# Chunk-selecting attention and a spatial gating unit on one core: dummy matmuls one by one, and a new table of order and engines

## The chip, the cores and the metric

The kernel runs on one core of a Trainium2 chip. The metric is the device time of one execution in microseconds. Engines are named as the profile names them: PE (TensorE's matmuls), PEld (its weight loads), DVE (VectorE), ACT (ScalarE), POOL (GpSimd), SP (SyncE, which here only issues DMAs).

## The reference

Attention in which each query looks at six chunks of 32 keys, picked by an upper bound of the score, followed by a gated MLP with a matrix over the sequence. Four batches, 8 heads, 768 positions, head width 64; MLP widths 512 and 1024.

```python
k_min = np.min(k_chunks, axis=3)
k_max = np.max(k_chunks, axis=3)
ub = np.sum(np.maximum(q * k_min, q * k_max), axis=-1)      # per query and chunk
ub = np.where(causal, ub, -1000000000.0)
top_chunks = np.argsort(ub, axis=-1)[..., -top_k:]
...
scores = np.where(sel & causal_positions, scale * q @ k.T, -1000000000.0)
attn = softmax(scores);  x = attn @ v                        # (4, 768, 512)
...
h = np.maximum(x @ w_in, 0.0)
u, v = h[..., :512], h[..., 512:]
v_n = (v - mean(v)) / np.sqrt(var(v) + 1e-06)
v_s = np.einsum('ts,bsd->btd', w_spatial, v_n) + b_spatial[None, :, None]
out = (u * v_s) @ w_out
```

Inputs and output are float32; the kernel computes in float16 with float32 sums.

## The kernel before

The work falls into 16 pairs of heads, numbered 0 to 15, four to a batch, and an MLP for each batch, numbered 0 to 3. Pairs 0 to 3 are cut into two halves of the sequence, `a` (rows 0 to 383) and `b` (384 to 767), so that work can start on the first half. Every step is an operation with a name: kind, pair (and half), and a number where there are several. Those that the text speaks of are:

- `ld_k4`, `ld_q0a`, `ld_wv2`: a load from HBM into a staging tile (`early` for the halves, `st` for the rest), issued by SP. `w_v` and `w_u` are the two halves of `w_in`, in four pieces each; `ws` is the matrix over the sequence.
- `c_k4`, `c_wv2`, `c_v6`: the cast of what was loaded to float16 (line 315, in a helper). `c_s10` copies a query once more, for pairs 10 to 15.
- `t_k4`, `e_k4`: six (for a half, three) transposes by PE (L562), and the copy of their result from PSUM into the tile `kqT` (L313 on ACT, L315 on DVE).
- `kmm0_4`, `kmm1_4`: greatest and least key of each chunk (L594, DVE); `km0_4`, `km1_4`: a copy of these for each of the two heads; `rq1_4`: the query's negative part (L612).
- `ub4`: the bounds, by PE (L629, L634); `max4`, `sel4`, `grd4`: the sixth greatest bound, the choice and a guard column; `tsel4`, `es4`: transpose and copy of the choice.
- `sc4_0` to `sc4_2`: scores with the mask added by PE (L746, L759, L767; L781 for pairs 10 to 15); `exp4_00` and so on: their exponentials (L795, ACT), two to a group; `tri4_00`: the causal edge (L806, POOL); `av4_0`, `av4_1`: attention times values (L829); `rec4_0`, `nrm4_0`: division by the sum.
- `tx0a`, `ex0a` or `xx5`: the attention's output transposed into `xT`, by PE or by a DMA. `x_kq10`, `xs10`, `xg0_1` are such transposing DMAs for other tiles.
- `v0_0`, `u0_0` (L878): the two projections of a tile of 128 rows; `rv`, `ru` (L885 on ACT, L887 on DVE) their relu; `bn`, `ag`, `ln`, `rs`, `vn` the normalisation; `s0_0` (L928) the product over the sequence; `g0_0` (L932, DVE) the gate; `o0_0` (L964) the output projection, `eo0_0` its copy from PSUM and `so0_0` its store. For the last tile of batch 3 the output is made in two pieces of 256 columns, `o3_5` and `o3_6`.
- `preset_...`: memsets of tiles that are filled once.
- `w0` to `w3`: dummy matmuls of 512 columns, whose result nobody reads (L454). The tile that they read is set to zero by `zero` (L409, DVE), and they write to the same two PSUM tiles `sc` as the scores.

Nothing is decided while the kernel is built: a table written out by hand, `ORDER`, names every operation in turn. The letter ahead of the colon is its engine (P for PE, D for DVE, A for ACT, G for POOL, S for SP), the digits behind it the buffers that it takes. `replay` walks through the table, and each engine's queue gets its operations in that order and runs them strictly one after the other; between engines only the data and the buffers make an operation wait. The list of engines that an operation may run on stands in its definition (`cast`, `evac`, `turned`).

`WARM` gives the dummies by operation: nine in `w0`, three in `w1`, five in `w2`, two in `w3`. In the table `w3` and `w2` stand first, `w1` behind the first two groups of transposes, and `w0` behind `t_k1b`, ahead of `tsel1a`.

Of the kernel before, what the change touches and what calls it, by code (L numbers as in the profile page):

```python
# [14 lines left out]
P = 128  # L15
# [15 lines left out]
def t_act(n):  # L31
    return n / 1.2 + 55.0


def t_pool(n):
    return n * 0.92 + 100.0
# [108 lines left out]
WARM = (9, 3, 5, 2)  # L145
# [25 lines left out]
max2aD:0 sc1a_0P:10 e_k0bA: e_q0bD: kmm0_0bD:2 sel2aD:0 preset_vt0D: km1_1bG: km0_1bA: km1_3aA: c_q2bA:3 grd2aA:
ub3aP:2 t_k2bP:0 tsel2aP:1 max3aD:1 ld_v2aS:7 ld_k4S:0 c_k4G:0 ld_k8S:1 ld_k3bS:8 ld_v1aS:2 es2aD:2 sel3aD:0 av0aP:3
e_k2bD: rec0aD:0 kmm1_0bD: t_q2bP:1 t_q1bP:2 kmm0_2bD:0 nrm0aD:0 kmm1_2bD: preset_sna1G: km1_0bG: grd3aG: km0_0bG:
c_k3bG:2 c_v1aG:2 ld_v3aS:0 c_v3aG:0 km0_2bG: exp1a_01A:1 exp1a_00A: rq1_0bA:0 c_q3bA:3 e_q2bA: e_q1bA: sc2a_0P:01
tsel3aP:0 t_q3bP:1 ub0bP:2 t_k4P:3 es3aD:3 e_q3bD: exp2a_01A:2 exp2a_00A: av1aP:0 max0bD:0 rec1aD:1 preset_vt1D:
c_v2aG:1 t_k3bP:1 e_k4A:4 grd0bA:1 km1_2bA: e_k3bA: sel0bD: nrm1aD:1 rq1_1bD:1 sc3a_0P:10 exp3a_01A:3 exp3a_00A:
tsel0bP:3 es0bD:4 kmm0_3bD:1 kmm1_3bD: tx0aP:2 tx1aP:0 ub1bP:1 av2aP:3 ex0aA:0 rq1_2bA:0 km0_3bG: rq1_3bD:1 rec2aD:2
max1bD:1 nrm2aD:0 sel1bD:1 ld_k5S:2 ld_v1bS:1 ld_wv0S:3 c_k5G:1 ld_wv3S:4 ld_k6S:5 c_wv0G:0 c_k6G:3 km1_3bG: ld_q4S:6
sc0b_0P:01 ex1aD: grd1bA: ub2bP:2 exp0b_01A:4 exp0b_00A: av3aP:3 t_k5P:1 tsel1bP:0 max2bD:0 kmm1_4D:2 rec3aD:0
sel2bD:1 nrm3aD:1 e_k5A:5 es1bD:0 c_q4G:0 c_k8G:2 ld_wv1S:7 c_wv1G: ld_wv2S:0 c_wv2G: c_wv3G: ld_wu2S:2 c_wu2G:0  # L180
ld_q6S:3 ld_q5S:5 ld_wu1S:6 ld_wu0S:1 ld_q8S:7 ld_wu3S:0 sc0b_1P:10 ub3bP:2 tx3aP:1 tx2aP:3 t_q4P:0 ex3aD: kmm0_4D:
t_k8P:1 exp0b_10A:5 exp0b_11A: grd2bA: e_k8A:0 e_q4D: preset_snb0G: ex2aD: max3bD:1 kmm1_5D:0 sel3bD:0 sc1b_0P:10
tsel2bP:0 v0_2P:1 v0_0P:3 exp1b_00A:6 exp1b_01A: km1_4A:1 grd3bG: km0_4G: rv0_0A:0 c_v1bG: tsel3bP:2 preset_sn0G:
c_q5G:1 tri1b_00G: rq1_4D:0 rv0_2A:1 es2bD:1 c_wu0G: es3bD:2 bn0_2D:0 sc1b_1P:10 ub4P:0 max4D:0 grd4G:2 c_wu3G:
c_q6G:0 c_wu1D: exp1b_10A:0 exp1b_11A: tri1b_10G: v0_1P:3 t_q5P:2 t_k6P:1 rv0_1A:2 e_k6A:1 preset_vt5D: sel4D: e_q5D:
bn0_0D:1 ld_k9S:4 c_k9D:2 ag0_2D:0 kmm0_5D: rq1_5D:1 sc2b_0P:10 u0_0P:3 u0_1P:0 t_q6P:1 exp2b_00A:1 exp2b_01A:
sc2b_1P:10 e_q6A: u0_2P:2 tsel4P:1 preset_vt4G: ru0_0D:0 es4D:3 exp2b_10A:2 exp2b_11A: ru0_1A:1 ld_ws4S:2 ld_v0bS:5
ld_ws0S:5 ld_k7S:1 av1bP:3 ld_v2bS:4 ld_ws1S:6 c_ws4A:1 km0_5G:2 tri2b_00G: c_k7G:3 km1_5G: tri0b_10G: tri2b_10G:
c_v2bG: tri0b_00G: epsG:0 sc3b_0P:10 exp3b_01A:3 exp3b_00A: t_k9P:1 c_v0bG: c_q8G:0 ld_q7S:0 c_q7G:2 ld_v3bS:6
ru0_2D:2 rec1bD:1 nrm1bD:1 kmm0_6D:1 bn0_1D:2 tx1bP:2 ub5P:0 max5D:1 av2bP:3 rec2bD:2 nrm2bD:0 ag0_1D: sel5D:0 e_k9A:2  # L190
ex1bA: sc3b_1P:01 exp3b_11A:0 exp3b_10A: t_k7P:1 t_q7P:3 t_q8P:2 av0bP:0 e_q8A: e_k7A:3 kmm1_6D: e_q7D: rec0bD:0
nrm0bD:1 kmm0_8D:2 rq1_6D:0 sc4_0P:10 tx2bP:3 ex2bD: ag0_0D: exp4_00A:6 exp4_01A: ld_ws2S:3 ld_wo0S:4 c_v3bG: c_ws1G:3
km0_6G:4 tri3b_00G: tri3b_10G: av3bP:2 tws4P:0 rec3bD:1 ld_ws3S:1 c_wo0G: km1_6G: grd5A: ld_v4S:2 c_v4G:5 tws1P:1
tx0bP:3 sc4_1P:10 ews4D:0 ex0bD: nrm3bD:0 c_ws0A:2 ln0_0A:0 ews1D: ld_ws5S:7 ld_q9S:0 ld_q11S:6 tri4_00G: c_ws5G:0
# [24 lines left out]
tri9_20G: sc10_0P:10 exp10_00A:6 v1_1P:1 av9_1P:3 av9_0P:2 rs1_1A: exp10_01A: ru1_3A:7 rv1_1A:3 sc10_1P:10 exp10_11A:0
# [55 lines left out]
def kernel(  # L275
# [760 lines left out]
```

## Time and profile before

| | us |
|---|---|
| median of three runs | 196.98 |
| lowest, highest | 196.94, 198.55 |
| the profiled execution, device time | 197.43 |
| its span, first to last instruction | 195.6 |
| PE busy in the span | 186.6 |
| DVE busy | 157.4 |
| ACT busy | 146.6 |
| POOL busy | 94.2 |

An engine's busy time counts its instructions on the engine; waiting, branching and issuing of DMAs is left out. Matmuls overlap one another, and the record of each holds its way through the array, so PE counts as busy while it is not at its full rate. A line such as L315 is that of a helper that many operations share.

### The profile page before, as it was taken

How to read it: one execution, taken by the hardware profiler on the slowest of the kernel's cores; microseconds unless marked ns; L12 is line 12 of the kernel's file. 1: busy time of each engine (PE TensorE's matmuls, PEld its weight loads, DVE VectorE, ACT ScalarE, POOL GpSimd, SP SyncE). 2: the span in 40 equal slices, each digit the busy share in tenths (PEclk: the TensorE clock that was granted, in tenths of full speed). 3: DMA queues.
4: the chain of work that ended last, by engine and by line, in shares of the span. 5: the costliest groups of instructions: out<-in, count | busy, mean ns of one | idle time of the engine just before them, and what ended most of it. 6: DMA issues, size and time to landing. Idle time of an engine off the chain costs nothing.

```text
span 195.6 us, 5812 instructions
## 1 busy us (share of the span) xinstructions
PE 186.6 (95%) x2201; PEld 107.9 (55%) x2201; DVE 157.4 (80%) x490; ACT 146.6 (75%) x231; POOL 94.2 (48%) x192
## 2 busy tenths in 40 slices
PE   7899979999999999999999999999999999999992
PEld 3457644576745646554357667566556654444441
DVE  5899988988998997995898997679947467895350
ACT  2699989999989997897999997788899330453142
POOL 4479469769688299932862674233615210000000
PEclk9999999999999999999999999999999999999999
DMA  5999899999999859999999989999171363812555
GB/s 145 326 336 285 282 302 278 323 350 352 275 227 220 137 135 245 190 244 179 257 212 225 264 161 159 272 261 218 57 167 57 80 138 107 229 41 111 165 180 192
DMA packets 98139, 41.01 MB, mean 210 GB/s; under 512 B 85440, under 2 KB 92864, under 8 KB 98112
## 3 DMA queue, kind: packets, MB, share of 16 engines
q1 hardware_dynamic: 97968, 40.52, 83.9%
q8 instruction: 17, 0.28, 0.6%
q10 hardware_dynamic: 144, 0.13, 0.2%
q14 instruction: 10, 0.08, 0.2%
HBM read 24.38 MB, written 6.29 MB: 157 GB/s over the span
## 4 chain that ended last, share of the span: by engine, by line
PE 69%; DMA 11%; POOL 8%; DVE 4%; issue 3%; SPq 2%; ACT 1%; POOLq 0%; ACTq 0%; DVEq 0%
PE gen L878 17%; PE gen L928 16%; PE gen L964 10%; PE gen L829 9%; PE sc L781 7%; DMA st<-in_moe_w_spatial_dram 5%; PE sc L746 4%; POOL n L315 3%; PE sc L759 3%; DMA early<-in_q_dram 2%; DMA early<-in_v_dram 2%; PE gen L629 2%; DMA st<-in_q_dram 1%; POOL vt L315 1%; SPq L515 1%
## 5 line engine op out<-in xcount | busy, mean ns | idle before, releaser
L795 ACT ACTIVATE e<-sc 128x768 f16<-128x768 f32 (+1 forms) x96 | 83.2, 916 | 12.6 <-PE sc L781 6.7
L806 POOL TENSOR_SCALAR_AFFINE_SELECT e<-e 128x512 f16<-128x512 f16 (+1 forms) x44 | 27.3, 630 | 23.2 <-ACT e L795 18.5
L928 PE MATMUL gen<-vn,wsT 128*128 128x512 f16 x144 | 34.2, 379 | 0.1
L594 DVE TENSOR_REDUCE kmm<-kqT 128x24 f16<-128x768 f16 (+1 forms) x40 | 30.3, 778 | 1.1 <-ACT kqT L313 1.1
L829 PEld LDWEIGHTS <-e 128*128 128x128 f16 x672 | 23.1, 97 | 4.3 <-issue 1.4
L932 DVE SCALAR_TENSOR_TENSOR late<-gen,bcol,u 128x512 f16<-128x512 f32 x24 | 17.7, 747 | 9.7 <-PE gen L928 9.7
L829 PE MATMUL gen<-vt,e 128*128 128x65 f16 x672 | 24.7, 193 | 0.6 <-DVE wsT L315 0.3
L964 PE MATMUL gen<-w_out,late 128*128 128x512 f16 (+1 forms) x100 | 23.8, 371 | 0.0
L928 PEld LDWEIGHTS <-wsT 128*128 128x128 f16 x144 | 13.3, 97 | 14.7 <-issue 0.6
L746 PE MATMUL sc<-kqT 64*128 64x128 f16 (+2 forms) x212 | 17.3, 271 | 0.6 <-ACT e L795 0.6
L896 DVE BATCH_NORM_STATS2 stats<-vraw 128x6 f32<-128x512 f32 x24 | 16.1, 684 | 1.8 <-ACT vraw L885 1.7
L313 ACT ACTIVATE late<-gen 128x512 f32<-128x512 f32 (+2 forms) x17 | 9.9, 587 | 9.6 <-PE gen L964 8.4
L781 PE MATMUL sc<-kqT,early 128*128 128x256 f16 (+2 forms) x132 | 16.7, 268 | 0.0
L885 ACT ACTIVATE vraw<-gen 128x512 f32<-128x512 f32 x14 | 8.2, 607 | 11.4 <-PE gen L878 11.3
L313 ACT ACTIVATE kqT<-gen 128x384 f16<-128x384 f16 (+1 forms) x21 | 12.6, 632 | 4.6 <-PE gen L562 4.4
L878 PEld LDWEIGHTS <-early 128*128 128x128 f16 x96 | 9.0, 98 | 10.8 <-issue 0.8
L656 DVE MAX8 max<-gen 128x8 f32<-128x20 f32 (+4 forms) x160 | 14.8, 166 | 0.0
L964 PEld LDWEIGHTS <-late 128*128 128x128 f16 x100 | 9.3, 97 | 9.6 <-issue 0.5
L878 PEld LDWEIGHTS <-xT 128*128 128x128 f16 x96 | 8.7, 97 | 9.2 <-issue 1.1
L315 POOL CAST n<-st 128x768 f16<-128x768 f32 x15 | 12.2, 824 | 3.2 <-ACT e L795 1.6
L781 PEld LDWEIGHTS <-early 128*128 128x128 f16 x132 | 10.9, 97 | 4.8
L885 ACT ACTIVATE u<-gen 128x512 f16<-128x512 f32 x17 | 10.1, 602 | 3.8 <-PE gen L878 3.8
(114 smaller groups left out, 340.6 us busy)
## 6 DMA issues: line engine op xcount, KB each, us to landing
out_dram<-late SPq DMA_DIRECT2D x23, 256.0 KB, 2.4
st<-in_k_dram SPq DMA_DIRECT2D x12, 384.0 KB, 4.9
st<-in_q_dram SPq DMA_DIRECT2D x12, 384.0 KB, 4.5
st<-in_v_dram SPq DMA_DIRECT2D x12, 384.0 KB, 4.3
st<-in_moe_w_spatial_dram SPq DMA_DIRECT2D x6, 384.0 KB, 5.5
st<-in_moe_w_in_dram SPq DMA_DIRECT2D x8, 256.0 KB, 5.4
early<-in_k_dram SPq DMA_DIRECT2D x8, 192.0 KB, 4.2
early<-in_q_dram SPq DMA_DIRECT2D x8, 192.0 KB, 4.4
```

The source lines that it names most:

```text
L313: e.activation(out=out, in_=in_, func=Act.Copy)
L315: e.tensor_copy(out, in_)
L594: lambda e, m=m, f=f, x=x, w=w: e.tensor_reduce(kmm.t[:, m, 0:nch], x().rearrange("d (c j) -> d c j", j=w), axis=AX.X, op=f, negate=(m == 1)),
L746: e.matmul(sc[z].t[:, a:a + len(qs) * P].rearrange("p (t c) -> p t c", c=P), lhsT=kq.t[r, 0, t * P:(t + 1) * P], rhs=qv[r, qs[0]:qs[-1] + ...
L781: e.matmul(sc[z].t[:, a:a + len(qs) * P].rearrange("p (t c) -> p t c", c=P), lhsT=st["kw"].t[:, hi, t // 2, t % 2 * P:(t % 2 + 1) * P], rh ...
L795: e.activation(out=e_.t[:, z, :, 0:w], in_=x.t.rearrange("p (h c) -> p h c", h=2)[:, :, 0:w], func=Act.Exp, scale=scale)
L806: e.affine_select(out=d, in_=d, compare_op=Alu.is_ge, fill=0.0, base=0, channel_multiplier=-1, pattern=[[0, 2 * len(zs)], [1, P]])
L829: e.matmul(avv()[:, n, hi, :], lhsT=es[g].t[:, zz, hi, c:c + P], rhs=vt.t[:, t, hi, 0:D + 1], start=(t == 0), stop=(t == qi))
L878: e.matmul(acc.t, lhsT=x.t[:, ko, t * P:(t + 1) * P], rhs=w.t[:, ko, :], start=(ko == 0), stop=(ko == NDO - 1))
L885: e.activation(dst.t, acc.t, func=Act.Relu)
L928: e.matmul(acc.t, lhsT=wsT.t[:, s, t * P:(t + 1) * P], rhs=vn[s].t, start=(s == 0), stop=(s == NQT - 1))
L964: e.matmul(acc.t[:, 0:w], lhsT=gT.t[:, a2 * KO + ko, :], rhs=w_out.t[:, ko, c0:c0 + w], start=(ko == 0), stop=(ko == KO - 1))
```

## The change

The dummies are issued otherwise, and the table is replaced as a whole.

```diff
-WARM = (9, 3, 5, 2)
+WARM = ((1,) * 14, (3,), (3,), (3,))
...
+DCAST = True
...
     def cast(n):
-        return {"POOL": t_pool(n), "DVE": t_dve(n, 2), "ACT": t_act(n) + 40.0}
-
-    for j, n in enumerate(WARM):
+        return {"POOL": t_pool(n), "DVE": t_dve(n, 2), "ACT": t_act(n) + 40.0} if DCAST else {"POOL": t_pool(n), "ACT": t_act(n) + 40.0}
+
+    for j, units in enumerate(WARM):
         waste = buf("sc")
-
-        def go(e, n=n, waste=waste):
-            for _ in range(n):
-                e.matmul(waste.t[:, 0:BANK], lhsT=zero[:, 0:P], rhs=zero, start=True, stop=True)
-        op(f"w{j}", {"PE": (234.0, 470.0, 250.0, 470.0)[j] * n}, go, reads=[(w_out, 0)], writes=[waste])
+        for i, n in enumerate(units):
+            def go(e, n=n, waste=waste):
+                for _ in range(n):
+                    e.matmul(waste.t[:, 0:BANK], lhsT=zero[:, 0:P], rhs=zero, start=True, stop=True)
+            op(f"w{j}_{i}", {"PE": 218.0 * n}, go, reads=[(w_out, 0)], writes=[waste])
```

There are 23 dummies instead of 19: fourteen operations of one (`w0_0` to `w0_13`) and three of three (`w1_0`, `w3_0`, `w2_0`). The other 1136 operations are the same. With `DCAST` true, casts may run on the same three engines as before. The beginning of PE's queue, before and after (the letter of the engine and the buffers left out):

```
before: w3 w2 t_k0a t_q0a w1 ub0a t_q1a t_k1a tsel0a t_k2a t_q2a sc0a_0 ub1a t_k3a t_q3a t_k1b
        w0 tsel1a t_k0b ub2a t_q0b sc1a_0 ub3a ...
after:  w0_0..w0_5 t_k0a w0_6 t_q0a w0_7..w0_10 t_k1a ub0a w0_11..w0_13 t_k2a t_q1a w1_0 tsel0a
        t_q0b t_k3a w3_0 t_q2a ub1a sc0a_0 tsel1a t_k0b t_k1b t_q3a ub2a w2_0 sc1a_0 tsel2a ...
```

The end of PE's queue, and the copies and stores that go with it:

```
before: ... s3_4 o3_0 o3_1 s3_5 o3_3 tg3_5 tg3_4 o3_2 o3_4 o3_6 o3_5   (last: eo3_5 on ACT, its store on ACT's queue)
after:  ... o3_1 o3_0 tg3_5 s3_4 o3_2 tg3_4 o3_6 o3_5 o3_4 o3_3       (last: eo3_6 eo3_5 eo3_4 so3_4 eo3_3 on ACT, so3_3 on SP)
```

Loads on SP's queue, in the order of issue:

```
before: k0a q0a k1a q1a k2a q2a k3a k1b q3a q1b k0b q0b q3b q2b k2b v0a v2a k4 k8 k3b v1a v3a k5 v1b
        wv0 wv3 k6 q4 wv1 wv2 wu2 q6 q5 wu1 wu0 q8 wu3 k9 ...
after:  k0a q0a k1a k2a q1a q0b k3a q2a q3a k0b k1b q1b q2b q3b k2b q4 v1a k6 k3b v3a k4 v2a k5 v0a
        wv3 q5 wv1 wu3 wv0 wu2 wv2 wu0 v0b wu1 k8 q6 v1b v3b v2b q9 k9 ...
```

128 operations run on another engine. Operations by engine, before and after: DVE 334 and 331, ACT 231 and 234, POOL 183 and 183, SP 133 and 133. Casts and copies named `c_`: DVE 7 and 12, ACT 13 and 9, POOL 64 and 63. On DVE they are `c_k0a c_q0a c_q1a c_wu1 c_k9 c_s11 c_v12` before, and `c_k0a c_q0a c_k2a c_wu3 c_wu2 c_q8 c_s11 c_v6 c_k13 c_s10 c_k12 c_v8` after. Other kinds: relu of the projections DVE 17 and 15, ACT 31 and 33; `rq` DVE 16 and 14, ACT 9 and 12, POOL 1 and 0; `km` POOL 30 and 28, ACT 10 and 12; `kw` POOL 6 and 8, DVE 4 and 4, ACT 2 and 0; presets DVE 8 and 6, POOL 14 and 16.

More of the change, by code (lines that the diff above doesn't have):

```diff
@@ new lines @@
+grd1aA: sc0a_0P:10 tsel1aP:2 t_k0bP:0 t_k1bP:1 es1aD:1 t_q3aP:3 ub2aP:2 exp0a_00A:0 exp0a_01A: w2_0P:1 sc1a_0P:10
+kmm1_3aD: preset_km0G: max2aD:0 e_k0bD: e_q3aA: sel2aD:0 kmm1_0bD:1 kmm0_0bD: rq1_3aD:1 e_k1bA: c_q1bG:3 km0_3aG:0
+c_k2bG:0 grd2aA: preset_snb1G: c_q2bG:2 tsel2aP:3 t_k2bP:0 t_q2bP:2 es2aD:2 e_k2bD: preset_vt1D: c_q4G:1 rq1_0bA:0
+km1_3aA: ub3aP:1 max3aD:1 km1_0bG: preset_vt0G: grd3aG:0 c_v1aG:5 t_q1bP:3 e_q1bD: sel3aD: kmm0_2bD:2 t_q4P:0
+kmm0_1bD:0 ld_k6S:1 ld_k3bS:7 c_k3bG:0 c_q3bG:2 km0_0bG: ld_v3aS:0 ld_k4S:2 c_v3aG:0 ld_v2aS:8 ld_k5S:3 ld_v0aS:1
@@ new lines @@
+rv0_2D:1 exp1b_01A:6 exp1b_00A: c_wu0G:0 grd3bA: c_wu3D: km1_4A:3 c_k8G:3 c_wu1G: km0_4G: c_wu2D: sc1b_1P:10
+exp1b_11A:1 exp1b_10A: c_v1bG: c_v0bG: v0_1P:2 tsel3bP:3 ub4P:0 t_k8P:1 rv0_1A:2 c_q6A:1 max4D:0 es3bD:2 kmm1_5D:2
+sel4D:0 sc2b_0P:01 exp2b_00A:2 exp2b_01A: e_k8A:1 u0_1P:2 av0bP:3 t_q6P:0 sc2b_1P:01 kmm0_5D: km0_5A:4 exp2b_10A:3
+exp2b_11A: u0_2P:1 tri1b_10G: preset_qs0G: grd4G: tri1b_00G: rec0bD:1 e_q6D: ru0_1D:0 nrm0bD:1 kmm1_6D:1 km1_5G:
+ru0_2A:1 tsel4P:0 av1bP:2 es4A:3 ld_ws2S:3 c_v3bG: c_v2bG: ld_q7S:4 ld_q8S:5 tri2b_10G: tri2b_00G: c_ws2G:2 c_k9G:0
@@ new lines @@
+so0_3S: kmm1_13D: rv1_3D:0 max11D:1 x_kq12S:3 kmm0_12D:2 bn1_3D:1 ag1_3D:2 ld_v10S:4 ld_v8S:3 sc9_1P:01 rv1_2A:1
+eo0_0A:0 exp9_10A:0 exp9_11A: v1_5P:3 v1_0P:2 u1_4P:0 sel11D: c_v8D:3 kw1_10G:0 rv1_5A:5 rq0_12A:0 bn1_5D:0 sc9_2P:01
+xs10S:1 ld_v9S:7 so0_2S: ld_k14S:2 xg0_5S:0 grd11G: tri8_20G: tri8_10G: preset_sn2D: rv1_0D:3 ag1_5D: bn1_0D:2
+tri9_10G: tri8_00G: kw0_10G: hold0_1G: exp9_21A:2 exp9_20A: c_v10G:4 hold0_0G: v1_4P:1 u1_1P:3 av8_1P:2 ru1_4A:6
+rv1_4A:4 ag1_0D:3 ru1_1D:7 tri9_20G: c_s12G:1 c_v9G:5 kmm1_12D: km0_12G:0 tri9_00G: rq1_13A:1 rq1_12D: sc10_0P:10
@@ new lines @@
+exp14_21A: o1_5P:1 av13_0P:3 sc15_0P:10 eo1_3A:1 eo1_5A:0 ag2_0D: vn2_4D:3 vn2_3D:4 ln2_0A:0 rs2_0A: vn2_2D:5 vn2_0D:0
+ru2_3A:8 vn2_5D:1 tri14_20G: vn2_1D:2 rec13_0D:1 av13_1P:2 av14_0P:1 rec14_0D:2 nrm13_0D: rec13_1D:0 nrm13_1D:
+exp15_01A:5 exp15_00A: c_v15G:4 o1_4P:0 sc15_1P:01 exp15_11A:0 exp15_10A: o1_2P:3 eo1_2A:2 s2_2P:2 sc15_2P:10
+av14_1P:3 g2_2D:0 rec14_1D:1 nrm14_0D:1 s2_0P:2 g2_0D:1 nrm14_1D: so1_5S: so1_2S: so1_3S: s2_1P:1 g2_1D: eo1_4A:0
+exp15_20A:2 exp15_21A: tri15_10G: hold1_0G: tri15_20G: tri15_00G: hold2_1G: s2_3P:0 g2_3D: av15_1P:2 rec15_1D:0
```

164 lines of the change are left out of this document (72 added, 92 removed).

## The prediction

> **What bounds the kernel now.** I read the page first, then a table of engine time by stretches, then the instructions of the first 14 us in order of time, then the chain of waits between 20 and 31 us and the end.
>
> ```profile
> span 195.6 us, 5812 instructions
> PE 186.6 (95%) x2201; PEld 107.9 (55%) x2201; DVE 157.4 (80%) x490; ACT 146.6 (75%) x231; POOL 94.2 (48%) x192
> ...
> PE 69%; DMA 11%; POOL 8%; DVE 4%; issue 3%; SPq 2%; ACT 1%; POOLq 0%; ACTq 0%; DVEq 0%
> ```
>
> TensorE is busy for 186.6 of 195.6 us and holds 69% of the chain that ends last; DMA, GpSimd and VectorE hold 23% of it. Where those sit is told by the stretches. Each row gives the length, then busy time with the number of instructions for TensorE's matmuls, its weight loads, VectorE, ScalarE and GpSimd, then the granted clock, the DMA share and GB/s.
>
> ```profile
> 0.00:5.00 5.00, 3.75 (x14) 1.83 (x15) 2.71 (x8) 1.50 (x2) 2.12 (x14) 1.00 0.54 148
> 5.00:14.00 9.00, 7.89 (x96) 4.54 (x96) 8.39 (x33) 7.20 (x17) 5.54 (x15) 1.00 1.07 331
> 14.00:22.00 8.00, 7.63 (x146) 5.66 (x143) 7.91 (x37) 7.91 (x19) 6.00 (x15) 1.00 0.99 280
> 22.00:30.00 8.00, 6.37 (x114) 3.90 (x111) 7.42 (x29) 7.13 (x12) 5.57 (x10) 1.00 0.91 304
> 30.00:45.00 15.00, 14.74 (x230) 8.94 (x226) 13.61 (x53) 14.66 (x20) 11.64 (x26) 1.00 1.03 324
> 45.00:65.00 20.00, 19.29 (x314) 12.33 (x308) 18.77 (x50) 18.86 (x32) 15.70 (x27) 1.00 1.04 254
> 65.00:95.00 30.00, 29.83 (x442) 15.81 (x438) 25.45 (x98) 25.70 (x37) 19.44 (x33) 1.00 0.98 197
> 95.00:190.00 95.00, 94.99 (x867) 53.76 (x860) 72.73 (x189) 61.98 (x97) 28.19 (x57) 1.00 0.74 165
> 190.00:196.00 6.00, 2.13 (x14) 1.17 (x12) 0.42 (x1) 1.67 (x4) 0.00 (x0) 0.91 0.47 175
> ```
>
> From 95 to 190 us TensorE is idle for 0.01 us: an order of work can gain nothing there, only lose. Its idle time is 2.36 us in the first 14 us (1.25 and 1.11), 2.00 us from 14 to 30 (0.37 and 1.63), and 1.14 us from 30 to 95 (0.26, 0.71, 0.17). From 14 to 65 us VectorE and ScalarE are busy for 89 to 99% of each stretch and DMA's share is 0.91 or more, so a TensorE that gets ahead there soon waits for one of them. So this change is worth what it does ahead of 95 us, and at the end behind TensorE's last matmul. The opening, in order of time (start, length):
>
> ```profile
> 1.25 3.17 PE L454 MATMUL sc<-w_out 128*128 128x512 f16 x7 [1.25 <-DVE w_out L409]
> 3.37 0.36 DVE L315 CAST n<-early 128x384 f16<-128x384 f32 x1 [0.49 <-DMA early<-in_k_dram]
> 4.21 0.85 PE L562 MATMUL gen<-ident,n 128*128 128x128 f16 x6
> 4.78 0.87 ACT L313 ACTIVATE kqT<-gen 128x384 f16<-128x384 f16 x2 [2.70 <-PE gen L562]
> 5.30 1.01 DVE L594 TENSOR_REDUCE kmm<-kqT 128x12 f16<-128x384 f16 x2 [1.07 <-ACT kqT L313]
> 5.47 0.50 POOL L315 CAST n<-early 128x384 f16<-128x384 f32 x1 [2.62 <-DMA early<-in_k_dram]
> 6.68 0.20 PE L629 MATMUL gen<-km,kqT 128*128 128x24 f16 x1 [0.34 <-ACT km L313]
> 7.04 0.56 PE L562 MATMUL gen<-ident,n 128*128 128x128 f16 x6
> 8.16 0.34 PE L702 MATMUL gen<-ident,snab 128*128 128x128 f16 x3 [0.56 <-POOL snab L668]
> 8.82 1.00 DVE L594 TENSOR_REDUCE kmm<-kqT 128x12 f16<-128x384 f16 x2
> 8.85 0.50 PE L746 MATMUL sc<-kqT 64*128 64x128 f16 x6
> 10.23 0.81 ACT L795 ACTIVATE e<-sc 128x768 f16<-128x768 f32 x1
> 10.26 0.19 PE L629 MATMUL gen<-km,kqT 128*128 128x24 f16 x1 [0.20 <-ACT km L313]
> 11.09 2.10 PE L454 MATMUL sc<-w_out 128*128 128x512 f16 x9
> 12.62 0.81 ACT L795 ACTIVATE e<-sc 128x768 f16<-128x768 f32 x1
> 13.88 0.34 PE L746 MATMUL sc<-kqT 64*128 64x128 f16 x4
> ```
>
> ```profile
> L454 PE MATMUL sc<-w_out x19: 376/610/635, 1.3 to 12.8; 128*128 128x512 f16 x19
> ```
>
> The last row is the dummies' line with the least, middle and greatest length of one in ns. They show TensorE's change of rate, though the clock column says 1.00 all through: seven take 3.17 us at 1.25, so they come (3.17 - 0.61)/6 = 0.43 us apart; nine take 2.10 us at 11.09, so (2.10 - 0.38)/8 = 0.215 apart. Six transposes take 0.85 us at 4.21 and 0.56 at 7.04, so the rate doubles near 7 us; slow transposes come some 0.11 us apart (an estimate from the 0.85).
>
> **The change part by part.** *Opening.* Both versions do the same real work ahead of the score group `sc1a_0`, which starts at 13.88; 19 dummies stand ahead of it before, 23 after. I follow the new order by hand with the lengths above. Six dummies from 1.25 end at 3.81; the first cast ends at 3.73, so the key's transposes run at 3.81 instead of 4.21, and ScalarE's copy, the two reductions of 1.01 us (5.30) and what follows come 0.4 us earlier. A seventh dummy and the query's transposes end at 4.88, then four slow dummies (4 x 0.43) at 6.59 and `t_k1a` at 6.91. The first bound `ub0a` stands behind them at 6.91, although its inputs could be there at 6.4 (the GpSimd cast of 5.47 + 0.50, then both copies `km` on GpSimd): 0.23 us later than 6.68. VectorE then does the second reduction straight behind the selection, with the copy `e_k1a` moved to ScalarE: about 8.2 instead of 8.82. `ub1a` still waits for the third query's cast on GpSimd: about 10.2 (10.26). The first scores now stand behind it, at about 10.4 instead of 8.85, and their first exponential starts near 11.8 (10.23 - 8.85 = 1.38 us behind them). Two of 0.81 us end at 13.4, and that releases `sc1a_0`: 0.4 us earlier than 13.88. The nine dummies of 11.09 no longer stand in a row; the last three end while the exponentials run, so they cost nothing as long as ScalarE is the late one. Bounds: 1.0 us gained if the four slow dummies run fast, 0.6 us lost if a cast on GpSimd comes late. I take -0.4.
>
> *From 14 to 30 us.* The chain of waits here (start, length, what):
>
> ```profile
> 24.23 2.73 DMA st<-in_q_dram
> 26.99 1.59 POOL n L315 x2
> 28.58 1.67 POOL w_v L315 x3
> ```
>
> The load of `q4` lands at 26.96, GpSimd casts it, then `k8`, then three pieces of `w_v`; the first projection starts as the last of these ends, near 30.2. The new order issues `ld_q4` 16th instead of 28th, and `k8` behind all weights. On SP's queue `q4` passes twelve loads, which issue one place later each; the last piece of `w_v` is the 31st load instead of the 30th. The wait for `q4` is gone. What comes next: ScalarE and VectorE, busy 7.91 of 8 and 7.13 and 7.42 of 8 us in these stretches, and DMA at 0.91 to 0.99. Bounds: 0 (they hold TensorE as much as before) and 2.0 us (all idle time gone). As the engines' rows are nearer to full than TensorE's, I take -0.6.
>
> *From 30 to 95 us.* Nothing is removed in kind; 128 operations change engine, and by number the engines end as they were (VectorE 334 to 331, ScalarE 231 to 234, GpSimd 183 to 183). Casts on VectorE go from 7 to 12, on ScalarE from 13 to 9, on GpSimd from 64 to 63.
>
> ```profile
> L315 DVE CAST vt<-st 128x768 f16<-128x768 f32 x1 | 0.6, 551 | 0.0
> L315 POOL CAST vt<-st 128x768 f16<-128x768 f32 x9 | 7.6, 848 | 0.2
> 6.49 0.23 DVE L420 TENSOR_SCALAR ex<-ones 128x24 f32<-128x24 f32 x1
> L403 DVE TENSOR_SCALAR first<-ident 128x8 f16<-128x8 f16 x1 | 0.8, 822 | 0.0
> ```
>
> A cast of 768 columns costs 551 ns on VectorE and 848 on GpSimd. Five that come to VectorE newly (`c_v6`, `c_k13`, `c_s10`, `c_k12`, `c_v8`) fall between 65 and 95 us: some 2.6 us more there, where it has 4.55 us idle. They delay the copies and reductions queued behind them on VectorE, which TensorE's next bound or score waits for. Bounds: -1.1 us (all idle time gone) to +2.6 us (all of them late). As 4.55 covers 2.6, I take 0.
>
> Against these casts the small operation `first` speaks: 822 ns, beside 0.23 us for a larger one of its kind; it ran while GpSimd wrote its presets. The Trainium skill (SBUF — State Buffer, "Who interferes with whom") says that a VectorE copy or cast in a two-port mode and a GpSimd operation exclude one another for a whole instruction. By that each moved cast could hold GpSimd for its 0.55 us too, and the sum would come out higher by what of 2.6 us GpSimd can't hide; it has 10.56 us idle from 65 to 95, so I leave it out of the sum.
>
> *The end.*
>
> ```profile
> 191.29 0.60 ACT L313 ACTIVATE late<-gen 128x512 f32<-128x512 f32 x1 [0.22 <-PE gen L964]
> 192.21 0.38 ACT L313 ACTIVATE late<-gen 128x256 f32<-128x256 f32 x1 [0.33 <-PE gen L964]
> 192.62 0.38 ACTq L971 DMA_DIRECT2D out_dram<-late  x1
> ```
>
> Before, the last matmuls make a tile of 256 columns, and ScalarE copies it in 0.38 us. After, they make `o3_3` with 512 columns (0.60 us), and ahead of that copy ScalarE issues the store `so3_4` (0.38 us, of which some 0.2 stick out past TensorE's end). So 0.22 + 0.2: +0.4 us, between 0.2 and 0.6.
>
> **Sum.** -0.4 - 0.6 + 0 + 0.4 = -0.6 us. The profiled execution took 197.43 us, 1.8 around its span of 195.6; so 196.8 by its own time, and 196.4 beside the median of 196.98 (196.94 to 198.55).
>
> **The rivals.** *The waits go and nothing takes their place* (faster). The 2.0 us of idle time from 14 to 30 and half of the 1.14 behind it go, with the opening's 0.4 gained and the end's 0.4 lost: 196.98 - 2.6 = 194.4. For it: the chain there runs over one late load and four casts, and both are moved. Against it: the full rows of ScalarE and DMA. *VectorE becomes the bound from 65 to 95 us* (slower). If its 4.55 us of idle time there are waits for results that the order can't fill, the five casts come on top: +2.6 - 0.6, so 199.0. It decides from the point at which less than 2.6 of the 4.55 can be used. For it: VectorE is 85% busy there and takes its work in order. Against it: the row of 95 to 190 shows that TensorE doesn't wait with VectorE at 77%. *The rate changes at another moment.* At 8.1 instead of near 7, two or three dummies more run slow and the opening's gain is lost: 196.8; if it changes some 2.5 us earlier, `ub0a` starts at 6.4 and 0.5 more is gained: 195.9. The Trainium skill (TensorE: Matmul & The Clock Gate, "What's actually happening") has the rate set by a free-running window of about 3.4 us and warns against fitting to a count of slow matmuls; by that an order made for one moment meets another in each run. No single trace can show that.
>
> **How the numbers follow.** Forecast 0.45 (its own range 195.4 to 197.9), waits gone 0.25, VectorE the bound 0.20, rate elsewhere 0.10. Over 1% faster is below 195.0, over 1% slower above 198.95; one per cent is about what a measurement of this kernel tells from no change. Faster: most of the 0.25 and a little of the forecast, 0.25. Slower: most of the 0.20 and a little of the rest, 0.20. Within: 0.55. The range takes in most of both sides, 194.2 to 199.1.
>
> **What would show it.** Right: `sc1a_0` near 13.4, the first exponential near 11.8; the first projection of `w_v` before 30 us and behind a copy by ScalarE rather than behind the load of `q4`; TensorE's idle time from 14 to 30 near 1.4 us, and next to none from 95 to 190; a last copy of 0.60 us that starts some 0.2 us behind TensorE's last matmul. Wrong: idle time of TensorE over 2 us from 65 to 95 with VectorE above 93%, waits for VectorE or for a transposing load beyond 95 us, or an opening in which scores start later than 10.8.

## The result, and the profile after

The changed kernel takes 195.44 us (median of ten runs, 195.26 to 196.63); the kernel before takes 196.70 in ten runs beside it. The ratio is 0.994, with a 95% interval of 0.991 to 0.997: faster, by less than one per cent. The forecast was 196.4 and "within 1%".

The page of the changed kernel (span, busy time by engine, and the chain that ended last by engine):

```profile
span 193.8 us, 5829 instructions
...
PE 185.9 (96%) x2205; PEld 107.6 (56%) x2205; DVE 155.8 (80%) x487; ACT 145.5 (75%) x234; POOL 93.9 (48%) x192
...
PE 77%; DVE 10%; ACT 5%; POOL 3%; DMA 2%; issue 2%; SPq 0%; ACTq 0%; POOLq 0%
```

DMA and GpSimd held 19% of the chain and now hold 5%; VectorE has come to 10%. The engines' busy time by stretches, with the same columns as before:

```profile
14.00:22.00 8.00, 7.33 (x134) 5.43 (x133) 7.96 (x33) 7.92 (x16) 6.67 (x19) 1.00 1.06 323
22.00:30.00 8.00, 7.59 (x129) 4.85 (x128) 7.93 (x35) 7.73 (x13) 6.74 (x17) 1.00 1.01 334
...
65.00:95.00 30.00, 29.82 (x401) 15.86 (x401) 28.72 (x94) 24.59 (x36) 14.01 (x26) 1.00 1.09 213
95.00:190.00 95.00, 94.94 (x864) 54.08 (x862) 67.73 (x181) 61.52 (x103) 30.13 (x55) 1.00 0.74 166
```

TensorE's idle time from 22 to 30 us fell from 1.63 to 0.41 and rose from 0.37 to 0.67 from 14 to 22. From 65 to 95 us VectorE is now busy for 28.72 of 30 us, and yet TensorE is idle for 0.18 there. The opening, in order of time:

```profile
1.25 2.74 PE L455 MATMUL sc<-w_out 128*128 128x512 f16 x6 [1.25 <-DVE km L439]
3.85 0.35 PE L563 MATMUL gen<-ident,n 128*128 128x128 f16 x3
4.57 1.03 PE L455 MATMUL sc<-w_out 128*128 128x512 f16 x4
5.97 0.50 POOL L316 CAST n<-early 128x384 f16<-128x384 f32 x1 [3.16 <-DMA early<-in_k_dram]
...
6.53 0.34 PE L563 MATMUL gen<-ident,n 128*128 128x128 f16 x3 [0.94 <-POOL n L316]
...
11.74 1.51 ACT L796 ACTIVATE e<-sc 128x768 f16<-128x768 f32 x2
12.86 0.81 PE L455 MATMUL sc<-w_out 128*128 128x512 f16 x3
13.60 0.50 PE L747 MATMUL sc<-kqT 64*128 64x128 f16 x6
16.64 0.50 PE L747 MATMUL sc<-kqT 64*128 64x128 f16 x6
```

Six dummies take 2.74 us, so they come 0.43 apart; the four at 4.57 take 1.03, 0.22 apart. The rate doubled near 3.9 us in this execution, ahead of the first transposes, and TensorE had used up the dummies ahead of `t_k1a` by 5.6 and stood idle until the second key's cast (6.53). The three dummies of `w2_0` run from 12.86 and end as `sc1a_0` starts. The last two rows are `sc1a_0` and `sc2a_0`; before, they started at 13.88 and 16.65. The end:

```profile
189.12 0.60 ACT L314 ACTIVATE late<-gen 128x512 f32<-128x512 f32 x1 [0.48 <-PE gen L965]
189.75 0.37 ACTq L972 DMA_DIRECT2D out_dram<-late  x1
190.24 0.60 ACT L314 ACTIVATE late<-gen 128x512 f32<-128x512 f32 x1 [0.52 <-PE gen L965]
```

TensorE's last matmul ends at 189.94 and the span at 193.81, 3.87 us later; in the kernel before they end at 192.13 and 195.64, 3.52 us apart (before rounding).

**Where the time came from.** The new order has its own sequence, so single times can't be set side by side. What can be is TensorE's lag: the start of an operation less the summed length of all useful matmuls ahead of it in TensorE's queue, as they follow one another in the trace at full rate (0.216 us for 512 columns, 0.056 for 128; dummies count as nothing). The profiled execution of the kernel before was 0.7 us above its median, so a second column sets the new kernel against `b_hold`, an experiment below with the old order and four dummies more, whose profiled execution took 196.32. Changes of the lag in us:

| stretch, by the new order's operations | new - before | new - `b_hold` |
|---|---|---|
| start to `sc1a_0` (13.6 us) | -0.28 | -0.26 |
| to `sc0b_0` (22.4) | +0.66 | +0.53 |
| to the first projection `v0_0` (29.2) | -1.62 | -1.11 |
| to `u1_3` (about 105) | -0.90 | -0.22 |
| to TensorE's last matmul | -0.05 | -0.05 |
| behind it, to the span's end | +0.35 | +0.35 |
| sum | -1.84 | -0.76 |

The medians lie between, at -1.26. The old order's executions spread more than the new one's. Of the 99 timings of the kernel before that came with the experiments, 18 have a granted clock of 0.990 or 0.991, which one window at half rate gives (the profiles of `b_newdum` and `b_q4b` below have 0.991 with one such window); their median is 197.09, that of the other 81 is 196.51. None of the ten timings of the new kernel is below 0.996. This is worth about 0.2 us at the median; why the rest of the old order's timings lie between 195.96 and 197.96 is open.

A part of the first column's fourth row is the profiled execution's own bad luck: these two waits of the kernel before for casts on GpSimd at 43 and 46 us have no counterpart in `b_hold`.

```profile
43.36 0.98 PE L829 MATMUL gen<-vt,e 128*128 128x65 f16 x27 [0.26 <-POOL vt L315]
...
45.98 0.23 PE L562 MATMUL gen<-ident,n 128*128 128x128 f16 x1 [0.38 <-POOL n L315]
```

### The profile page after: what moved, and what is told of

Its sections match the earlier page's. It is cut to its first block, busy times and chain, and to the rows that moved or that the text cites. A ratio compares the mean times of both kernels' runs of the same rounds, so it can differ in the third digit from the quotient of the medians.

```text
span 193.8 us, 5829 instructions
## 1 busy us (share of the span) xinstructions
PE 185.9 (96%) x2205; PEld 107.6 (56%) x2205; DVE 155.8 (80%) x487; ACT 145.5 (75%) x234; POOL 93.9 (48%) x192
## 4 chain that ended last, share of the span: by engine, by line
PE 77%; DVE 10%; ACT 5%; POOL 3%; DMA 2%; issue 2%; SPq 0%; ACTq 0%; POOLq 0%
PE gen L879 19%; PE gen L929 16%; PE gen L965 10%; PE gen L830 9%; PE sc L782 7%; PE sc L747 5%; PE sc L760 3%; PE gen L630 2%; DMA early<-in_k_dram 2%; PE gen L563 2%; ACT e L796 2%; DVE kmm L595 2%; DVE max L657 2%; POOL n L316 1%; ACT kqT L314 1%
## 5 line engine op out<-in xcount | busy, mean ns | idle before, releaser
L807 POOL TENSOR_SCALAR_AFFINE_SELECT e<-e 128x512 f16<-128x512 f16 (+1 forms) x44 | 27.4, 632 | 24.3 <-ACT e L796 16.6
L886 ACT ACTIVATE vraw<-gen 128x512 f32<-128x512 f32 x17 | 10.1, 604 | 12.1 <-PE gen L879 12.1
L782 PE MATMUL sc<-kqT,early 128*128 128x128 f16 (+2 forms) x132 | 16.7, 267 | 0.0
L911 DVE TENSOR_SCALAR vn<-vraw,mv,rstd 128x512 f16<-128x512 f32 x24 | 13.0, 590 | 3.2 <-ACT rstd L906 3.2
L316 POOL COPY km<-kmm 64x48 f16<-64x48 f16 (+1 forms) x28 | 5.9, 212 | 16.5 <-DVE kmm L595 14.6
```

Source lines behind the costliest of these rows:

```text
L782: e.matmul(sc[z].t[:, a:a + len(qs) * P].rearrange("p (t c) -> p t c", c=P), lhsT=st["kw"].t[:, hi, t // 2, t % 2 * P:(t % 2 + 1) * P], rh ...
L807: e.affine_select(out=d, in_=d, compare_op=Alu.is_ge, fill=0.0, base=0, channel_multiplier=-1, pattern=[[0, 2 * len(zs)], [1, P]])
```

## The experiments

Two theories stood at the start: the gain comes from the dummies and an earlier full rate (theory 1), or from the new order (theory 2), above all from the earlier load of `q4` (2a). Theories 3 to 5 came as these fell. The kernel before, timed beside each group, had medians of 196.5 to 196.8. The new kernel's 195.44 is compared across groups on that ground.

**No dummies, in both orders (`a_none`, `b_none`).** In both, `WARM` is emptied and the dummies' words leave the table.

```diff
-WARM = ((1,) * 14, (3,), (3,), (3,))
+WARM = ()
```

> The changed kernel with all 23 dummy matmuls left out (they compute nothing that is read); the table is otherwise the same. Theory 1, the gain comes from the dummies: without them TensorE changes its rate later than at 3.9 us, the transposes and scores of the opening run at half rate, sc1a_0 starts after 14.2 (13.60 with them) and the time is 196.2 to 197.5. Theory 2, the gain comes from the order: sc1a_0 waits for the two exponentials and not for TensorE, so it starts at 13.6 +-0.4 and the time is 195.2 to 195.9.

> The kernel before with all 19 dummy matmuls left out (they compute nothing that is read). With a_none it gives what the order alone is worth. Theory 2 (the order carries the gain by itself): 1.0 to 1.6 us slower than a_none's 197.44, so 198.4 to 199.0. Theory 3 (order and dummies were fitted to each other; the old order needs its dummies as much as the new one): without them it loses about the 2.0 us that the new order lost, so 198.3 to 199.2 as well, and TensorE stays at half rate to 14 us or beyond. Against both (the old order needs no dummies): 196.5 to 197.5, level with a_none.

Measured: 197.44 (196.72 to 198.03) in the new order, so the dummies are worth 2.0 us there; 197.69 (196.83 to 199.30) in the old one, where they are worth about 0.9. Theory 3 asked for 198.3 to 199.2 in the old order, so that order needs its dummies less than the new one does. Without any, the two orders differ by 0.25 in their medians, within their spread. In `a_none` (the key's transposes, and two groups of scores, `sc1a_0` and `sc2a_0`):

```profile
3.78 0.99 PE L562 MATMUL gen<-ident,n 128*128 128x128 f16 x6 [3.78 <-DVE n L315]
...
13.99 0.79 PE L746 MATMUL sc<-kqT 64*128 64x128 f16 x6
...
17.69 0.50 PE L746 MATMUL sc<-kqT 64*128 64x128 f16 x6
```

Six matmuls of scores take 0.79 us at 14 and 0.50 at 17.7: TensorE stays at half rate to about 14.6. `sc1a_0` is late by 0.39, `sc2a_0` by 1.05 us, and from there the kernel stays 0.9 to 1.2 late to its end. By the start of `sc1a_0` theory 2 is nearer, by the time theory 1: the price is paid behind `sc1a_0`. Theory 2's 1.0 to 1.6 us for the order alone aren't there either; the new order's gain shows only together with its dummies.

**The dummies exchanged (`a_olddum`, `b_newdum`).** New order with the old dummies, old order with the new ones (TensorE's queue):

```diff
 a_olddum
+w3 w2 t_k0a t_q0a w1 t_k1a ub0a ... ub1a sc0a_0 w0 tsel1a ...
 b_newdum
+w0_0..w0_5 t_k0a w0_6 t_q0a w0_7..w0_10 ub0a w0_11..w0_13 t_q1a t_k1a w1_0 tsel0a t_k2a t_q2a
+w3_0 sc0a_0 ub1a t_k3a t_q3a t_k1b tsel1a t_k0b ub2a t_q0b w2_0 sc1a_0 ...
```

> The changed kernel's order with the 19 dummies of the kernel before at their old places (two and five ahead of t_k0a, three behind t_q0a, nine ahead of tsel1a). Theory 1 (dummies): the first key's transposes start at 4.2 again instead of 3.85, sc1a_0 starts at 13.9 or later, the time is 196.2 to 196.8, no better than before. Theory 2 (order): the nine run while ScalarE works on the exponentials, sc1a_0 starts at most 0.3 us later than 13.60, the time is 195.3 to 195.9.

> The kernel before, its order unchanged, with the 23 dummies of the changed kernel at the corresponding places of its own queue. Theory 1 (dummies): 0.5 to 1.0 us below the kernel before, 195.7 to 196.2, and sc1a_0 well ahead of 13.88. Theory 2 (order): within 0.4 us of the kernel before, whatever sc1a_0 does, since the projections of w_v still wait for q4's load until 30.1.

Measured: 199.19 (197.69 to 200.75) and 197.67 (197.12 to 198.71), so both are slower than either kernel. Neither theory had room for that. Both fall into two groups by the granted clock: in `a_olddum` three executions at 0.998 and above take 197.69 to 198.33 and three at 0.978 to 0.983 take 200.05 to 200.75; in `b_newdum` five at 0.988 to 0.991 take 198.47 to 198.71, and of the seven at 0.997 and above six take 197.12 to 197.30 and one 198.04. The profile of `a_olddum` is of the first group, that of `b_newdum` of the group at 0.991. In `a_olddum`:

```profile
12.54 2.10 PE L455 MATMUL sc<-w_out 128*128 128x512 f16 x9 [0.79 <-ACT e L796]
...
15.61 0.50 PE L747 MATMUL sc<-kqT 64*128 64x128 f16 x6
```

The nine dummies write to a tile `sc`, and in the new order both are taken by the first scores until ScalarE has read them: the nine start at 12.54 and hold `sc1a_0` back to 15.61. This is a fault of the exchange, not the price of the old dummies as such. In `b_newdum` (rows by time, then one stretch, with the granted clock as the third column from the end):

```profile
13.43 0.39 PE L704 MATMUL gen<-ident,snab 128*128 128x128 f16 x2 [0.97 <-DVE snab L686]
14.52 1.49 PE L456 MATMUL sc<-w_out 128*128 128x512 f16 x3
15.94 0.82 PE L748 MATMUL sc<-kqT 64*128 64x128 f16 x6
```

```profile
13.50:16.80 3.30, 3.30 (x33) 1.67 (x33) 2.59 (x12) 2.17 (x6) 3.17 (x7) 0.50 1.03 329
```

The old order has its nine dummies in a gap between 11 and 13 us. Without them TensorE waited there, fell back to half rate from 13.48 to 16.89 by the clock's record, and `sc1a_0` started at 15.94 instead of 13.88. That is the group of 198.5; the other group, at 197.2, is still 0.5 us slower than the 196.71 of the kernel before beside it, and no profile shows why. So order and dummies don't combine freely, and their shares don't add.

**Fewer and more dummies (`a_14`, `b_hold`).**

```diff
 a_14
-WARM = ((1,) * 14, (3,), (3,), (3,))
+WARM = ((1,) * 14,)
 b_hold
-WARM = (9, 3, 5, 2)
+WARM = ((9,), (4,), (5,), (2,), (3,))        # the last three ahead of tsel0a
```

> The changed kernel without the last three groups of three dummies (w1_0, w3_0, w2_0, from 7 to 13.5 us); the fourteen single ones stay. Theory 4, the later dummies hold the rate: once in full rate by 4 to 7 us, TensorE falls back to half rate for a window of 3.41 us between 7 and 14 us in some or all executions, and the time is 0.5 to 1.5 us longer, 196.0 to 197.0, or falls into two groups 0.8 or more apart. Rival, only the early change counts: within 0.2 us of the changed kernel, 195.3 to 195.7.

> The kernel before with four dummies more: four instead of three behind t_q0a, and three ahead of tsel0a, in the gaps of 1.1 and 0.56 us that TensorE has there at full rate. Theory 4 (what the dummies of the change do is to hold the rate in every execution, wherever the windows fall): the spread of the kernel before (195.96 to 198.17 over 32 runs) narrows to 1.2 or less and the median falls by 0.3 to 0.7, to 196.0 to 196.5. Rival, the order alone: median and spread as before, 196.6 to 197.0.

Measured: 195.49 (195.12 to 195.98) without the last nine, level with the new kernel, so theory 4 falls: in the new order the dummies behind the fourteenth do nothing for the time. `b_hold` takes 196.43 (196.06 to 197.79), which lies in theory 4's range, but the kernel before has 196.51 beside it, and the spread is not narrower: nothing gained either. In `a_14` `sc1a_0` starts at 12.96, 0.64 us ahead of the new kernel, and `sc2a_0` at 16.66:

```profile
11.76 1.51 ACT L796 ACTIVATE e<-sc 128x768 f16<-128x768 f32 x2
12.96 0.70 PE L747 MATMUL sc<-kqT 64*128 64x128 f16 x6
...
16.66 0.50 PE L747 MATMUL sc<-kqT 64*128 64x128 f16 x6
```

Before, in the new kernel and here `sc2a_0` starts between 16.64 and 16.66: what the opening gains by 13 us is gone by 16.6. The exponentials of `a_14` run when those of the new kernel do, to within 0.02 us, and `sc1a_0` starts before the second ends (13.27). So it was `w2_0` that held `sc1a_0` to 13.60 in the new kernel, and not the exponentials.

**q4's load early in the old order (`b_q4`, `b_q4b`).**

```diff
-ld_q4 28th of the loads
+ld_q4 16th, behind ld_k2b      (b_q4)
+ld_q4 24th, behind ld_k5       (b_q4b)
```

> The kernel before with one word moved: ld_q4 is issued 16th instead of 28th. Theory 2a, the wait for this load is what the new order saves between 14 and 30 us: the load lands near 14 instead of 26.7, the first projection starts near 29.2 instead of 30.1, TensorE's idle time from 22 to 30 falls from 1.63 to near 0.7, and the time falls by 0.5 to 1.0. Rival 2b, the load isn't what counts (the last pieces of w_v land at 28.2 and are cast in a row behind k8, and ScalarE and VectorE are full): the first projection starts at 29.7 or later, the time falls by less than 0.4.

> The kernel before with ld_q4 issued 24th instead of 28th, behind the four loads of values and k5, so that no load of values is later than before (issued 16th it put them 0.8 us late, and TensorE waited 0.70 us at 19.4 for them). Theory 2a (which load is late decides from 14 to 30 us): q4 lands near 21.1, the waits near 27.5 and 28.2 go (0.31 and 0.42 us) and none of that size comes at 19.4; 0.4 to 0.8 us below the kernel before. Rival 2b (ScalarE, VectorE and DMA are full there and take its place): within 0.3 us of the kernel before.

Measured: 197.01 (ratio to the kernel before 1.003, 1.001 to 1.004) and 197.16 (1.001, 0.999 to 1.003). Theory 2a falls. The waits of `b_q4` over 0.3 us between 17 and 31 us:

```profile
18.46 0.34 PE L702 MATMUL gen<-ident,snab 128*128 128x128 f16 x3 [0.63 <-POOL snab L668]
20.09 0.52 PE L829 MATMUL gen<-vt,e 128*128 128x65 f16 x12 [0.54 <-POOL vt L315]
26.60 0.40 PE L746 MATMUL sc<-kqT 64*128 64x384 f16 x4 [0.47 <-ACT e L795]
30.32 0.33 PE L702 MATMUL gen<-ident,snab 128*128 128x128 f16 x3 [0.36 <-DVE kqT L315]
```

Issued 16th, the load puts those of the values back, and TensorE waits for a value's cast (20.09) instead. At 30.3 it waits for VectorE's copy of q4's own transposes, `e_q4`: these still stood in TensorE's queue just ahead of the projections and held a PSUM tile. In `b_q4b` the waits are alike (0.52 us lost at 29.7), and its profiled execution also fell back to half rate between 8.45 and 11.87 us.

**q4's whole chain late in the new order (`a_q4late`).** The load, the cast, the transposes and their copy together:

```diff
-ld_q4 16th; c_q4, t_q4 and e_q4 (ACT) done by 17.6 us; ub3b in PSUM buffer 0
+ld_q4 27th, ld_wu3 behind ld_v0b; c_q4 between c_wv0 and c_wv2; t_q4 ahead of sc1b_0; e_q4 on DVE behind kmm0_4; ub3b in buffer 2
```

> The changed kernel with the chain of q4 put back to where the kernel before has it: the load 27th instead of 16th (in the place of a piece of w_u, which goes three places back), its cast on GpSimd between the pieces of w_v, its transposes straight ahead of sc1b_0 and the first projections, and their copy on VectorE. Theory 5 (what stood in TensorE's queue ahead of the first projections made the gain between 25 and 30 us): TensorE waits 0.5 us or more for the cast or the copy between 25 and 31 us, and 0.5 to 1.0 us of the gain are lost, 195.9 to 196.5. Rival (q4's chain doesn't matter, the rest of the order carries the gain): no new wait over 0.3 us there, 195.2 to 195.7.

Measured: 197.47 (197.11 to 198.34), 2.0 us more than the new kernel and twice the upper end of what theory 5 allowed. The transposes of q4, VectorE's copy of them, and the third projection, `v0_1`:

```profile
28.22 0.51 PE L564 MATMUL gen<-ident,n 128*128 128x128 f16 x6 [0.77 <-POOL n L317]
...
31.47 0.95 DVE L317 COPY kqT<-gen 128x768 f16<-128x768 f16 x1
...
34.02 1.02 PE L880 MATMUL gen<-w_v,xT 128*128 128x512 f16 x4 [1.48 <-DVE snab L686]
```

TensorE waits 0.77 us for GpSimd's cast of q4. Its lag is 1.1 us above the new kernel's at `sc1b_0`, right behind, but 0.6 at the first projection, `v0_0`, mostly because the new kernel waits for an exponential within `sc1b_0` (28.13) and this one doesn't. So 0.6 us is what theory 5 can claim here, about half of the 1.1 gained between 22 and 29 us against `b_hold`; what made the other half is not shown. The rest of the loss, 1.5 us, is a second wait that the edit made itself. The copy stands in VectorE's queue ahead of `sel3b` (L686), which must read the bounds of `ub3b` before their PSUM tile is free; and the edit, which needs a tile for `t_q4`, gives `ub3b` the tile that `v0_1` takes next (buffer 2 instead of 0). So `v0_1` waits 1.48 us for `sel3b`, and that doesn't belong to the old order.

**The five casts back (`a_casts`).**

```diff
-c_v6 c_k13 c_k12 c_v8 c_s10   D
+c_v6 c_k13 c_k12 c_v8         G
+c_s10                         A
```

> The changed kernel with the five late casts back where they were (c_v6, c_k13, c_k12, c_v8 on GpSimd, c_s10 on ScalarE). Theory 2 (VectorE had the room and nothing waits for it): within 0.3 us of the changed kernel, 195.2 to 195.8, while VectorE's busy time from 65 to 95 us falls from 28.7 to about 26.1. Rival, the casts on VectorE cost (TensorE waits for VectorE, or VectorE and GpSimd hold each other up): 0.5 us or more faster, below 194.9. Other rival, the casts are what gained from 65 to 95: slower by 0.3 to 1.0, 195.8 to 196.5.

Measured: 196.24 (195.79 to 197.22), 0.8 us slower than the new kernel; against the kernel before 0.998 (0.997 to 1.000), where the new one has 0.994. Up to `sc9_0` at 89.1 the two profiles agree within 0.1 us; then, in `a_casts`:

```profile
94.27 0.82 POOL L316 CAST vt<-st 128x768 f16<-128x768 f32 x1 [1.73 <-DMA st<-in_v_dram]
...
96.29 2.40 POOL L807 TENSOR_SCALAR_AFFINE_SELECT e<-e 128x512 f16<-128x512 f16 x4
...
98.75 0.87 PE L830 MATMUL gen<-vt,e 128*128 128x65 f16 x23 [0.37 <-POOL e L807]
```

and in the new kernel:

```profile
93.93 2.71 POOL L807 TENSOR_SCALAR_AFFINE_SELECT e<-e 128x512 f16<-128x512 f16 x4
95.21 0.94 DVE L316 CAST vt<-st 128x768 f16<-128x768 f32 x1
```

On GpSimd the cast `c_v8` waits 1.73 us for its load, and the causal edges (L807) queued behind it start at 96.29 instead of 93.93; TensorE waits for them, and `sc10_0` comes 0.56 us later. Of the five, `c_v8` is the only one whose place shows in TensorE's times. VectorE's busy time from 65 to 95 us is 27.53 us here and 28.72 in the new kernel: 1.2 less and not 2.6, partly since `c_v8` runs at 95.2. TensorE's idle time from 95 to 110 us is 0.37 us in `a_casts`, 0.00 in the new kernel:

```profile
95.00:110.00 15.00, 14.63 (x178) 8.94 (x176) 13.24 (x41) 13.97 (x26) 10.59 (x21) 1.00 1.15 212
```

It is 0.00 in the kernel before as well, which has `c_v8` on GpSimd. So VectorE's idle time took the casts, and the move of `c_v8` spares the new order a loss of 0.5 us by the profiles, 0.8 by the medians, that the old order didn't have; it is no gain over the old order.

**The end turned round (`a_tail`, `a_tail2`).** TensorE's last operations:

```diff
-tg3_5 s3_4 o3_2 tg3_4 o3_6 o3_5 o3_4 o3_3
+tg3_5 s3_4 o3_2 tg3_4 o3_3 o3_4 o3_6 o3_5      (a_tail)
+tg3_5 s3_4 o3_2 tg3_4 o3_6 o3_3 o3_4 o3_5      (a_tail2; eo3_4 on DVE, so3_4 on SP)
```

> The changed kernel with the end turned round: the pieces o3_3 and o3_4 of 512 columns ahead of the two of 256, so the last copy is a short one and ScalarE issues no store ahead of it. The term of +0.36 us for the end goes: 0.3 us below the changed kernel's 195.44, so 195.0 to 195.3, with 3.5 us instead of 3.87 from TensorE's last matmul to the end of the span. If the new end was hidden by something else: 195.4 to 195.6.

> The changed kernel with another end that spares the two waits of a_tail (a copy waiting 2.1 us for an output tile whose store had been queued late, and TensorE waiting 0.58 us for a copy): one piece of 256 columns stands ahead of o3_3 and o3_4, the other behind them; o3_4 is copied by VectorE and stored by SP, the last copy is 0.38 us. If the end of the new order costs its 0.36 us: 0.2 to 0.35 us below the changed kernel's 195.44, so 195.1 to 195.25. If an output tile's store is what ends last: 195.4 to 195.8.

Measured: 197.52 (196.75 to 198.26) and 196.18 (195.39 to 197.40); neither beats the new kernel. Five of the twelve executions of `a_tail2` take 195.39 to 195.56, level with it, and the profiled one is among the two longest (197.37). In `a_tail`:

```profile
188.10 2.76 PE L965 MATMUL gen<-w_out,late 128*128 128x512 f16 x16 [0.58 <-DVE late L316]
189.93 0.60 ACT L314 ACTIVATE late<-gen 128x512 f32<-128x512 f32 x1 [2.11 <-DMA out_dram<-late]
```

There are three output tiles; with two stores queued behind a third, the copies waited 2.11 us for one to come free, and TensorE waited 0.58 us ahead of `o3_3` for the copy out of the PSUM tile of `tg3_4`. In `a_tail2` the first is mended, but `o3_3` still waits 0.31 us for that tile, and the end behind TensorE's last matmul shrinks by only 0.15 us, to 3.72. Its profile also has a wait that no other profile of the new order has:

```profile
34.71 0.18 PE L630 MATMUL gen<-km,kqT 128*128 128x48 f16 x1 [0.89 <-POOL km L316]
```

GpSimd's queue stood still for 1.71 us ahead of the cast of `k8`, which ran at 32.71 instead of 30.36, and `km0_4` stands behind it. The edit lies 150 us later, so this belongs to the execution and not to the new end.

The term itself is borne out by the profiles: behind TensorE's last matmul come 3.49 to 3.53 us in the six profiles of the old order and 3.85 to 3.88 in the six of the new whose end is as in the change.

## Why the prediction came out right, step by step

**The time and the class.** 195.44 lies in the range and in the forecast's own range of 195.4 to 197.9, at its lower edge. The forecast said -0.6 and the medians say -1.26. Against `b_hold` the lag gives -0.76, and there the terms come out near what was forecast: -0.26 for the opening (-0.4), +0.53 - 1.11 = -0.58 from 14 to 30 us (-0.6), some -0.2 beyond (0), +0.35 for the end (+0.4). Against the profiled execution of the kernel before they are -0.28, -0.96, -0.9 and +0.35. What the medians have beyond 0.76 is mostly that other executions of the old order take longer than the one profiled in `b_hold` (196.32, against the median of 196.70), for which the sum has no term. That the terms agree so well is in part luck, as the next two show.

**The opening, -0.4.** `sc1a_0` came at 13.60 and the first exponential at 11.74, as worked out to 0.2 and 0.1 us. But the step "that releases `sc1a_0`" is wrong: the three dummies of `w2_0` held it to 13.60, and without them it starts at 12.96, before the exponentials have ended (`a_14`). The step was also carried to the end of the sum: `sc2a_0` stands still at 16.6 however early `sc1a_0` is, and by 22 us the new kernel's lag is 0.3 to 0.4 us larger. The working for `ub0a` was right for another reason than given: it came at 7.01 not behind slow dummies, which were fast from 3.9 us on, but because the second key's cast started at 5.97 instead of 5.47, and the copies `km` behind it on GpSimd.

**14 to 30 us, -0.6.** The net size is about right (-0.58 or -0.96), but it is made of two parts that the sum doesn't have: the opening's lead is lost by 22 us (+0.53 or +0.66), and from 22 to 29 us more is gained (-1.11 or -1.62). The reason "as the engines' rows are nearer to full than TensorE's" doesn't carry the second part: from 22 to 30 us VectorE and ScalarE are busy for 7.93 and 7.73 of 8 us (before 7.42 and 7.13, in `b_hold` 7.76 and 7.84), and TensorE's idle time went to 0.41 all the same (before 1.63, in `b_hold` 1.01). A full row told only that the engine was busy, not that TensorE waited for it. TensorE's idle time from 14 to 30 came to 1.08 us, where 1.4 was foretold. "The wait for `q4` is gone" is right, but it isn't the load's place alone that does it (`b_q4`, `b_q4b`); the chain's place in the queues does a part (`a_q4late`, 0.6 us by the first projection). The chain of waits of the new kernel from 27 us on shows the exponentials, and then TensorE alone to the first projection:

```profile
27.03 1.05 ACT e L796
...
28.13 0.39 PE sc L747 x4
...
29.22 1.90 PE gen L879 x8
```

The first projection starts at 29.22, ahead of 30 as foretold; what stands in front is ScalarE's exponential, not its copy.

**30 to 95 us, 0.** By the columns -0.9 or -0.2, and 0.64 us of the first are the two waits at 43 and 46 us. "As 4.55 covers 2.6" held: VectorE took the casts, and TensorE is idle for only 0.18 us from 65 to 95. What the sum didn't ask is what the casts would have held up on GpSimd in the new order; `a_casts` shows it for `c_v8`, 0.5 to 0.8 us. The Trainium skill (SBUF — State Buffer, "Who interferes with whom") has a cast of VectorE in a two-port mode and a GpSimd operation exclude one another; the trace fits that in one place, where `c_v8` takes 0.94 us instead of some 0.55 while GpSimd's four edges take 2.71 instead of 2.40. Leaving it out of the sum was right: TensorE is idle for 0.00 us from 95 to 110.

**The end, +0.4.** Measured +0.35, and +0.33 to +0.39 over all pairs of profiles.

**The rivals.** *The waits go and nothing takes their place* came nearest in its mechanism: most of TensorE's idle time from 22 to 30 us did go, but that from 14 to 22 rose by 0.30. *VectorE becomes the bound* had its premise come true, 28.72 of 30 us busy, and not its consequence; its bound of +2.6 fell with `a_casts`, which is slower with less on VectorE. *The rate changes at another moment* didn't decide: by the clock's record the rate doubled at 3.91 us in the profile of the new kernel, 5.02 in `a_14`, 6.00 in `a_tail` and 7.08 in `a_casts`, and `sc2a_0` started at 16.64, 16.66, 16.94 and 16.57. The Trainium skill (TensorE: Matmul & The Clock Gate, "What's actually happening") says that the window runs free of the kernel; the moments bear that out. The new opening takes it within 0.4 us; the rival's +0.4 and -0.5 don't show.

## What to carry to other kernels

Dummy matmuls and the order of the real work are one design: exchanged between the two orders here they cost 1.0 us (`b_newdum`) and 3.75 us (`a_olddum`) at the median. In the two profiles, the new dummies left open a gap that the old order fills with its own, and the old ones waited for a PSUM tile of the new order's scores and held the next scores back. In queues that run strictly in order, ask of every step that waits for a load what stands behind it on the same engine: q4's chain (0.6 us) and `c_v8` (0.5 to 0.8, within the new order) are such steps moved to where nothing urgent is behind them, and a load issued earlier without the rest of its chain gained nothing. Read a full row of an engine as busy, not as what is waited for, and set a profile that lies 0.7 us above its median against a second one before its small waits are counted.

## What the runs showed of the hardware

The column of the granted clock says 1.00 for the opening in every profile up to the first change, though matmuls there come 0.43 us apart at first and 0.22 later: the record starts with the first change, so a half rate at the start has to be read from the matmuls. Twice the rate was halved again in the middle of the opening, for one window (3.41 us in `b_newdum`, at 0.50; the same length in `b_q4b`), and it came back by itself. In the 3.41 us ahead TensorE had been idle for 1.47 us in `b_newdum` and 1.51 in `b_q4b`, in gaps of less than 1 us; windows with 1.31 us (`a_olddum`, from 4.81) and 1.35 us (`a_tail2`, from 3.96) of idle time were not followed by a fall. The small operation `first`, 0.82 us beside GpSimd's memsets of 0.42 us before, took 0.17 us after, beside the end of one of 0.12 us:

```profile
2.75 0.17 DVE L404 TENSOR_SCALAR first<-ident 128x8 f16<-128x8 f16 x1 [1.50 <-POOL ident L386]
```
